# Bias and tap vectors loaded as rows and turned by TensorE, the last MLP tile column done half by half, and the diagonal matrices built later on VectorE, in a fused SSM-convolution and token-MLP kernel

## The chip, the cores and the metric

The kernel runs on one core of one Trainium2 chip (trn2). The metric is the device time of one execution in microseconds (us), lower is better. Before the change the median of three runs was 204.59 us (204.25 to 204.87). All results were correct against the reference. The profiled span is the time from the first to the last instruction; the device time is 1.9 us longer than the span (205.34 against 203.4 for the profile of before), so a microsecond of span is a microsecond of time.

## The reference, cut to what matters

```python
# S = 2048, D = 640, F = 1536, bf16
k_shift = sum over 4 taps of k_pad[:, t:t+S, :] * shift_k[:, 3-t]
kv      = k_shift * v
y       = causal convolution of kv with ssm_k over S (rfft, product, irfft) + kv * ssm_D
a       = q * y
h       = layernorm(x)             # x = q
b       = (gelu(h^T @ w1 + b1) @ w2 + b2)^T
g       = sigmoid((x * gate_w).sum(-1))
out     = g * a + (1 - g) * b
```

The small tensors of the change are `shift_k` (640 x 4 taps), `b1` (1536), `b2` (2048) and `gate_w` (640).

## The kernel before

The transforms are matrix products with a sine table `FTB`. TensorE first transposes `ssm_k` (`ident,ssm`), then transforms it (`wT,FTB`), makes the shifted `k` by products with diagonal matrices of the taps (`DG,KT`), transforms the products `k_shift * v` (`vkv,FTB` for the first half of the sequence, `kv,FTB` for the second), and does the MLP (`X,ring`, then `GT,W`) between and after these. ScalarE moves results out of PSUM. VectorE does layernorm, the products and the additions between transforms. GpSimd has two small operations for each group of four layernorm tiles. There are four PSUM slots.

No order is written down: operations are added to a list scheduler inside the program, with modelled durations, and it decides, once, when the program is built, in which order each engine gets its instructions. The chip runs the engines asynchronously in this fixed order. So a small edit (another assumed DMA rate) can move instructions on every engine.

The small loads, and the product that makes `DG`:

```python
for hk in range(2):
    ssm_load(hk)
small(gwb[:, :], dr(gate_w, 0, [[0, 128], [1, D]]), 128 * 1280, "QA")            # QA: ScalarE's DMA queue
small(shk[:, :, :], dr(A_shift_k, 0, [[4, 128], [512, ND], [1, 4]]), 5120, "QA", noncontig=True)
small(Drow[:, :], dr(A_ssm_D, 0, [[0, 1], [1, D]]), 1280, "QA")
for hk in range(4):
    x_load(hk)
ssm_load(2)
ssm_load(3)
small(b1t[:, :], dr(B_b1, 0, [[1, 128], [128, FT]]), 3072, "SP", noncontig=True, chain=True)
small(b2t[:, :].rearrange("p (a b) -> p a b", a=4), dr(B_b2, 0, [[4, 128], [512, 4], [1, 4]]), 4096, "SP", noncontig=True, chain=True)
# ... w1, k transposes ...
tt("DVE", DG[:, :, :, :].rearrange("p a b c -> p (a b) c"), V(ident, 0, [[0, 20], [1, 128]]), V(shk, 0, [[1, 20], [0, 128]]), ALU.mult, mode=1)
```

Layernorm for one group of four tiles (`STATS_ACT` groups, whose sums ScalarE makes, cut):

```python
def ln_tile(hk, p):
    t = 4 * hk + p
    xs = X[:, hk, p, :]
    # bn_stats twice, bn_aggr -> mv[:, t, :]            (DVE)
    stt("DVE", junk[1][:, :], xs, 1.0, gwb[:, :], ALU.mult, ALU.mult, acc=gpre[:, t:t + 1])   # the gate's sum

def ln_apply(hk):
    r = slice(4 * hk, 4 * hk + 4)
    ts("POOL", vtmp[:, r], mv[:, r, 1], 1e-5, None, ALU.add)
    tt("POOL", rstd[:, r], vtmp[:, r], V(cst, 1, [[0, 4]]), ALU.pow)
    for p in range(4):
        ts("DVE", X[:, hk, p, :], X[:, hk, p, :], mv[:, t, 0:1], rstd[:, t:t + 1], ALU.subtract, ALU.mult, mode=4, extra=0.17)

for h in range(2):
    # ... transposes and transforms of ssm half h ...
    for kt in range(2):
        for p in range(4):
            ln_tile(2 * h + kt, p)
        ln_apply(2 * h + kt)
    if h == 0:
        mixing(C[0], SS, 0, fine=True)       # additions between transforms, DVE
    else:
        mixing(C[1], C[0], 0)
```

The second MLP product, and the output of a pair of tiles:

```python
for p in range(4):
    vt = _VT("mlp")
    for a in range(3):
        items = []
        for ft in range(4 * a, 4 * a + 4):
            for ci in range(2):
                items.append((chk(ci), V(W2h, ft * 512 + p, [[4, 128]]), GT[:, ft, 320 * ci:320 * ci + 320], ft == 0, ft == FT - 1))
        mms(vt, items, prio=2 * 10 ** 6 + 4 * (4 * n_ + p) + a, name="m2")
    act(O1[:, hk, p, :].rearrange("p (a b) -> p a b", a=2), two, ACT.Identity, bias=c2[:, t:t + 1], scale=omg[:, t:t + 1], vt=vt, name="o1")
# ...
tt("DVE", ov, cg[:, :, :], ov, ALU.add)
dma(dr(out, (1024 * h + p) * D, [[4 * D, 128], [512 * D, 2], [1, D]]), ov, 256 * 1280, sem="out")
```

## Time and profile before

| | before (first profile) |
|---|---|
| time, median of 3 runs | 204.59 us |
| time of the profiled execution | 205.34 us |
| span of the profiled execution | 203.4 us |
| first matmul | 7.38 us |
| statistics begin on VectorE | 11.66 us |
| second-half kv transform begins on TensorE | 79.13 us |
| TensorE unbroken | 68.91 to 199.0 us |
| from TensorE's end to the span's end | 4.4 us |

From the page of the profile of before: busy time of the engines, the DMA rate in 40 equal slices (one is 5.1 us), and the chain that ended last.

```profile
PE 187.5 (92%) x1374; PEld 136.8 (67%) x1374; DVE 183.0 (90%) x202; ACT 103.2 (51%) x143; POOL 20.8 (10%) x25
...
GB/s 104 355 401 213 311 200 210 198 358 297 183 253 58 0 3 0 0 73 168 174 0 45 265 2 124 163 373 195 196 258 214 366 80 0 48 141 73 0 193 68
...
PE 86%; ACT 8%; DMA 3%; issue 0%; DVE 0%
```

TensorE (PE) and VectorE (DVE) are busy for almost the same time, 187.5 and 183.0 us. The chain says which of the two the end waited for: TensorE, for 86% of the span. VectorE appears in it only with the last addition (0.82 us), but with 183 us of work it cannot be far behind; the chain shows the last constraint and not the second to last. The fourth slice, 213 GB/s among slices of 355 and 401, is the time of the 2- and 8-byte elements of `b1` and `b2`.

The end of the chain of waits of before, in order of time (start, length, what):

```profile
65.97 1.28 ACT L651
...
67.27 0.79 ACT GT L651
...
68.17 0.60 ACT C_84 L651
...
68.91 130.09 PE pp L293 x960
...
199.02 0.89 ACT O_99 L651
...
199.93 0.82 DVE O_99 L613
```

TensorE's last stop before its long run ends at 68.91: it waits for a PSUM slot behind ScalarE's table load (1.28 us at 65.97) and what follows it. From there 960 recorded matmuls run without a gap, 130.09 / 960 = 0.1355 us each. Whatever comes after 68.91 on TensorE is full, so the end can only move if TensorE's last stop ends earlier, if fewer matmuls lie behind that stop, or if the tail (here ScalarE's eviction of 0.89, VectorE's addition of 0.82, and the output's transfer) gets shorter.

The timeline of before around the second-half kv transform (start, length, engine, line, operation, out<-in):

```profile
75.87 3.42 PE L293 MATMUL pp<-X,ring_80 128*128 128x320 bf16 x24
76.98 1.48 DVE L613 TENSOR_TENSOR kv_93<-ksh_95,v_92 128x2560 bf16<-128x2560 bf16 x1
...
79.13 1.11 PE L293 MATMUL pp<-kv_93,FTB 128*128 128x320 bf16 x7
```

VectorE's second kv product ends at 78.46, and TensorE reaches the transform that reads it at 79.13. So VectorE has a lead of 0.67 us here.

The timeline of before around the second layernorm group:

```profile
26.08 1.43 DVE L613 TENSOR_TENSOR SS<-C_82 128x2560 bf16<-128x2560 bf16 x1
...
26.25 1.35 POOL L623 TENSOR_SCALAR vtmp<-mv 128x4 f32<-128x4 f32 x1 [4.97 <-DVE mv L817]
27.69 1.04 POOL L613 TENSOR_TENSOR rstd<-vtmp,cst 128x4 f32<-128x4 f32 x1
...
28.77 1.51 DVE L624 TENSOR_SCALAR X<-X,mv,rstd 128x640 bf16<-128x640 bf16 x4 [1.25 <-POOL rstd L613]
```

The bracket is idle time ahead of an instruction and who ended it: VectorE waits 1.25 us for GpSimd's `rstd`.

### The profile page before, as it was taken

Reading aid. Unit: us, or ns where it says so; the run is one execution under the profiler, and the core shown is the slowest. Engines: PE = TensorE matmul, PEld = TensorE weight load, DVE = VectorE, ACT = ScalarE, POOL = GpSimd, SP = SyncE. Lnnn points to the kernel's source line nnn. Section 1 sums busy time; section 2 is a strip of 40 time slices with the busy share of each in tenths; the row PEclk is TensorE's granted clock in tenths of the full one; section 3 lists DMA queues with packets and bytes.
Section 4 is the critical chain, followed back from the end, with each engine's and each line's share of the span. In section 5 each row is a group of like instructions: output and inputs, shape, how many; then the busy total and the mean of one; then the engine's idle time right before and its main releaser. Section 6 shows DMA issues by size and latency. Waiting matters only on the chain.

```text
span 203.4 us, 3261 instructions
## 1 busy us (share of the span) xinstructions
PE 187.5 (92%) x1374; PEld 136.8 (67%) x1374; DVE 183.0 (90%) x202; ACT 103.2 (51%) x143; POOL 20.8 (10%) x25
## 2 busy tenths in 40 slices
PE   0479989999998999999999999999999999999991
PEld 0446556577654677777777777788888887777770
DVE  8799979998997999999999999999999992799651
ACT  4697988966378765883111211131322314643741
POOL 1002040402043500000000004004000000000000
PEclk9999999999999999999999999999999999999999
DMA  4998999999891000025501807995996920142051
GB/s 104 355 401 213 311 200 210 198 358 297 183 253 58 0 3 0 0 73 168 174 0 45 265 2 124 163 373 195 196 258 214 366 80 0 48 141 73 0 193 68
DMA packets 37904, 32.37 MB, mean 159 GB/s; under 512 B 18305, under 2 KB 35330, under 8 KB 37890
## 3 DMA queue, kind: packets, MB, share of 16 engines
q1 hardware_dynamic: 36000, 29.37, 49.4%
q0 software_dynamic: 1088, 2.62, 8.2%
q10 hardware_dynamic: 802, 0.17, 0.6%
q8 instruction: 11, 0.18, 0.3%
q14 instruction: 3, 0.02, 0.0%
HBM read 23.25 MB, written 2.62 MB: 127 GB/s over the span
## 4 chain that ended last, share of the span: by engine, by line
PE 86%; ACT 8%; DMA 3%; issue 0%; DVE 0%
PE pp L293 86%; DMA ssm<-in_A_ssm_k_dram 3%; ACT wT L651 3%; ACT C_84 L651 2%; ACT FTB L651 1%; ACT C_82 L651 1%; ACT L651 1%; ACT O_99 L651 0%; DVE O_99 L613 0%; ACT GT L651 0%; ACT gth L651 0%
## 5 line engine op out<-in xcount | busy, mean ns | idle before, releaser
L293 PE MATMUL pp<-X,ring_80 128*128 128x320 bf16 x256 | 36.9, 299 | 0.0
L293 PEld LDWEIGHTS pp<-X,ring_80 128*128 128x128 bf16 x256 | 25.0, 98 | 9.7
L651 ACT ACTIVATE O_99<-pp,c_66,omg 128x640 bf16<-128x640 f32 x16 | 14.2, 884 | 34.1 <-PE pp L293 34.1
L293 PE MATMUL pp<-GT,W_1_98 128*128 128x320 bf16 x192 | 27.2, 299 | 0.0
L293 PE MATMUL pp<-GT,W_0_97 128*128 128x320 bf16 x192 | 26.4, 299 | 0.0
L651 ACT ACTIVATE GT<-pp,b1f 128x640 bf16<-128x640 f32 x12 | 9.5, 794 | 30.6 <-PE pp L293 30.6
L293 PEld LDWEIGHTS pp<-GT,W_0_97 128*128 128x128 bf16 x192 | 21.8, 114 | 4.3
L293 PEld LDWEIGHTS pp<-GT,W_1_98 128*128 128x128 bf16 x192 | 21.7, 114 | 4.5
L293 PE MATMUL pp<-wT,FTB 128*128 128x320 bf16 x128 | 20.8, 321 | 0.1
L293 PE MATMUL pp<-X,ring_81 128*128 128x320 bf16 x128 | 17.6, 299 | 0.0
L293 PEld LDWEIGHTS pp<-wT,FTB 128*128 128x128 bf16 x128 | 11.9, 104 | 8.3 <-ACT C_83 L651 1.7
L293 PE MATMUL pp<-ident,ssm 128*128 128x128 bf16 x80 | 8.5, 266 | 8.5 <-DMA ssm<-in_A_ssm_k_dram 7.4
L293 PEld LDWEIGHTS pp<-X,ring_81 128*128 128x128 bf16 x128 | 12.5, 98 | 4.9
L815 DVE BATCH_NORM_STATS2 stats<-X 128x6 f32<-128x320 bf16 x32 | 13.7, 466 | 0.0
L293 PEld LDWEIGHTS pp<-ident,ssm 128*128 128x128 bf16 x80 | 6.6, 129 | 10.4 <-DMA ssm<-in_A_ssm_k_dram 8.0
L651 ACT ACTIVATE C_84<-pp 128x640 bf16<-128x640 f32 x16 | 10.5, 701 | 5.1 <-PE pp L293 5.1
L631 DVE SCALAR_TENSOR_TENSOR junk_75<-X,gwb 128x640 bf16<-128x640 bf16 x16 | 12.9, 808 | 0.0
L651 ACT ACTIVATE C_85<-pp 128x640 bf16<-128x640 f32 x16 | 10.1, 708 | 4.1 <-PE pp L293 4.1
L293 PE MATMUL pp<-vkv_91,FTB 128*128 128x320 bf16 x64 | 10.6, 301 | 1.1 <-ACT C_84 L651 1.1
L651 ACT ACTIVATE wT<-pp 128x640 bf16<-128x640 f32 x16 | 10.0, 730 | 2.2 <-PE pp L293 2.2
L651 ACT ACTIVATE C_82<-pp 128x640 bf16<-128x640 f32 x16 | 10.1, 735 | 1.9 <-PE pp L293 1.9
L651 ACT ACTIVATE C_83<-pp 128x640 bf16<-128x640 f32 x16 | 9.9, 774 | 0.6 <-PE pp L293 0.6
(103 smaller groups left out, 301.9 us busy)
## 6 DMA issues: line engine op xcount, KB each, us to landing
ring_80<-in_B_w_dram SPq DMA_DIRECT2D x8, 512.0 KB, 5.2
W_0_97<-in_B_w_dram SPq DMA_DIRECT2D x4, 768.0 KB, 9.5
W_1_98<-in_B_w_dram SPq DMA_DIRECT2D x4, 768.0 KB, 8.0
ssm<-in_A_ssm_k_dram SPq DMA_DIRECT2D x4, 640.0 KB, 10.5
X<-in_A_q_dram SPq DMA_DIRECT2D x4, 640.0 KB, 10.3
out_dram<-O_99 SPq DMA_DIRECT2D x8, 320.0 KB, 2.3
ring_81<-in_B_w_dram SPq DMA_DIRECT2D x4, 512.0 KB, 8.9
vkv_91<-in_A_v_dram SPq DMA_DIRECT2D x2, 640.0 KB, 5.7
```

Of the source, the lines that this page charges most:

```text
L293: ins = self.nc.tensor.matmul(ps_ap, lhsT=lhsT, rhs=rhs, start=start, stop=stop, skip_group_check=True)
L631: eng, lambda e: e.scalar_tensor_tensor(out=o, in0=a, scalar=sc, in1=b, op0=op0, op1=op1, accum_out=acc),
L651: return T.op("ACT", lambda e: e.activation(o, src, func, **kw), rr + [src], ww)
L815: SC.add("DVE", 0.46, (lambda o, i: lambda s: T.op("DVE", lambda e: e.bn_stats(o, i), [i], [o]))(o, i), [i], [o])
```

## The change

Its intent: the tiny-element loads of `b1`, `b2` and the taps become a few contiguous rows that TensorE transposes (nine small matmuls into one PSUM slot, one eviction to `cc`). `gwb` (160 KB) leaves the head of ScalarE's DMA queue and goes behind the first X block. `DG` is built from `cc`, no longer ahead of all statistics but behind those of the eighth tile, ahead of the first mixing. The assumed DMA rate of the scheduler goes from 280 to 320. The last MLP column is computed half by half, so that less is left to do after the last matmul. Cut to its core:

```diff
-        def dma(o, i, nbytes, stream="SP", prio=None, sem=None, rate=280.0, chain=False, **kw):
+        def dma(o, i, nbytes, stream="SP", prio=None, sem=None, rate=320.0, chain=False, **kw):
 ...
-        small(gwb[:, :], dr(gate_w, 0, [[0, 128], [1, D]]), 128 * 1280, "QA")
-        small(shk[:, :, :], dr(A_shift_k, 0, [[4, 128], [512, ND], [1, 4]]), 5120, "QA", noncontig=True)
         small(Drow[:, :], dr(A_ssm_D, 0, [[0, 1], [1, D]]), 1280, "QA")
-        for hk in range(4):
+        small(rows[0:5, 0, :], dr(A_shift_k, 0, [[512, 5], [1, 512]]), 5120, "QA")
+        small(rows[0:4, 1, :], dr(B_b2, 0, [[512, 4], [1, 512]]), 4096, "QA")
+        small(rows[0:12, 2, 0:128], dr(B_b1, 0, [[128, 12], [1, 128]]), 3072, "QA")
+        x_load(0)
+        dma(gwb[:, :], dr(gate_w, 0, [[0, 128], [1, D]]), 128 * 1280, chain=True)
+        for hk in range(1, 4):
             x_load(hk)
         ssm_load(2)
         ssm_load(3)
-        small(b1t[:, :], dr(B_b1, 0, [[1, 128], [128, FT]]), 3072, "SP", noncontig=True, chain=True)
-        small(b2t[:, :].rearrange("p (a b) -> p a b", a=4), dr(B_b2, 0, [[4, 128], [512, 4], [1, 4]]), 4096, "SP", noncontig=True, chain=True)
 ...
-        tt("DVE", DG[:, :, :, :].rearrange("p a b c -> p (a b) c"), V(ident, 0, [[0, 20], [1, 128]]), V(shk, 0, [[1, 20], [0, 128]]), ALU.mult, mode=1)
+        vt = _VT("cv")
+        items = []
+        for j in range(4):
+            items.append(((lambda s, j=j: s[:, 5 * j:5 * j + 5]), V(rows, j, [[4, 128]], pn=5), ident[0:5, 0:5], True, True))
+        for p in range(4):
+            items.append(((lambda s, p=p: s[:, 20 + 4 * p:24 + 4 * p]), V(rows, 512 + p, [[4, 128]], pn=4), ident[0:4, 0:4], True, True))
+        items.append(((lambda s: s[:, 36:48]), rows[0:12, 2, 0:128], ident[0:12, 0:12], True, True))
+        mms(vt, items, name="cst")
+        act(cc[:, :], lambda s: s[:, 0:48], ACT.Copy, vt=vt, name="cc")
 ...
             if h == 0:
+                tt("DVE", DG[:, :, :, :], V(ident, 0, [[0, 5], [0, 4], [1, 128]]), shkf, ALU.mult, mode=1)
                 mixing(C[0], SS, 0, fine=True)
 ...
+                last_ = n_ == 3 and p == 3
+                order = [(ft, ci) for ci in range(2) for ft in range(FT)] if last_ else [(ft, ci) for ft in range(FT) for ci in range(2)]
 ...
+                    if last_:
+                        act(O1[:, hk, p, 320 * a:320 * a + 320], chk(a), ACT.Identity, bias=c2[:, t:t + 1], scale=omg[:, t:t + 1], vt=vt, name="o1")
 ... (the last pair of output tiles: addition and output DMA in pieces)
```

What the diff does not show is what the scheduler makes of it. Comparing the instruction orders of the two kernels: on TensorE one 14-matmul piece of the second-half `DG,KT` products goes ahead of the first-half (`vkv`) transforms; these 64 matmuls, which had MLP matmuls between them, become one block; and 48 instead of 80 MLP matmuls lie ahead of the second-half kv transform.

More of the change, by code (lines that the diff above doesn't have):

```diff
@@ L555, in _build @@
         DG = alloc("DG", [128, ND, 4, 128], BF16)
-        shk = alloc("shk", [128, ND, 4], BF16)
+        cc = alloc("cc", [128, 48], F32)
         stats = alloc("stats", [128, 16, 12], F32)
@@ L566, in _build @@
         c2 = alloc("c2", [128, 16], F32)
-        b2t = alloc("b2t", [128, 16], BF16)
-        b1t = alloc("b1t", [128, FT], BF16)
-        b1f = alloc("b1f", [128, FT], F32)
         cst = alloc("cst", [128, 2], F32)
@@ L589, in _build @@
         ksh = [alloc(f"ksh{i}", [128, 4, D], BF16, at=base_of(GT) + 5120 * (1 + i)) for i in range(2)]
+        rows = alloc("rows", [12, 3, 512], BF16, at=base_of(GT))
         pint = alloc("pint", [128, 4, 2, 2, 256], I32, at=base_of(ring[1]))
@@ L759, in _build @@
                 scale=-(2.0 * math.pi / 4096.0) * (1.0 - 1e-6), name="sin")
-        tt("DVE", DG[:, :, :, :].rearrange("p a b c -> p (a b) c"), V(ident, 0, [[0, 20], [1, 128]]), V(shk, 0, [[1, 20], [0, 128]]), ALU.mult, mode=1)
+        vt = _VT("cv")
[7 more added lines that the diff above has]
+        act(cc[:, :], lambda s: s[:, 0:48], ACT.Copy, vt=vt, name="cc")
+        b1f = cc[:, 36:48]
+        b2f = V(cc, 20, [[1, 4], [4, 4]])
+        shkf = V(cc, 0, [[1, 5], [5, 4], [0, 128]])
         def transp(h, p, kt):
@@ L847, in _build @@
                 mixing(C[1], C[0], 0)
-        SC.add("POOL", 0.3, lambda s: T.op("POOL", lambda e: e.tensor_copy(b1f[:, :], b1t[:, :]), [b1t[:, :]], [b1f[:, :]]), [b1t[:, :]], [b1f[:, :]])
         gate_op = act(gth[:, :], gpre[:, :], ACT.Tanh, scale=0.5)
@@ L852, in _build @@
         ts("POOL", omg[:, :], gth[:, :], -0.5, 0.5, ALU.mult, ALU.add)
-        tt("POOL", c2[:, :], omg[:, :], b2t[:, :], ALU.mult)
+        tt("POOL", c2[:, :].rearrange("p (a b) -> p a b", a=4), omg[:, :].rearrange("p (a b) -> p a b", a=4), b2f, ALU.mult)
         memset("POOL", KT[0][:, :, 12:16], 0.0)
@@ L925, in _build @@
                 mms(vt, items, prio=10 ** 6 + 4 * ft + hk, name="m1")
-            g_ = act(GT[:, ft, :].rearrange("p (a b) -> p a b", a=2), two, ACT.Gelu_apprx_tanh, bias=b1f[:, ft:ft + 1], vt=vt, prio=0, name="gelu")
+            g_ = act(GT[:, ft, :].rearrange("p (a b) -> p a b", a=2), two, ACT.Gelu_apprx_tanh, bias=cc[:, 36 + ft:37 + ft], vt=vt, prio=0, name="gelu")
             if ft == 0:
@@ L945, in _build @@
                 t = 4 * hk + p
-                for a in range(3):
+                last_ = n_ == 3 and p == 3
+                order = [(ft, ci) for ci in range(2) for ft in range(FT)] if last_ else [(ft, ci) for ft in range(FT) for ci in range(2)]
+                na = 2 if last_ else 3
+                for a in range(na):
                     items = []
-                    for ft in range(4 * a, 4 * a + 4):
-                        for ci in range(2):
-                            items.append((chk(ci), V(W2h, ft * 512 + p, [[4, 128]]), GT[:, ft, 320 * ci:320 * ci + 320], ft == 0, ft == FT - 1))
+                    for ft, ci in order[a * (24 // na):(a + 1) * (24 // na)]:
+                        items.append((chk(ci), V(W2h, ft * 512 + p, [[4, 128]]), GT[:, ft, 320 * ci:320 * ci + 320], ft == 0, ft == FT - 1))
                     mms(vt, items, prio=2 * 10 ** 6 + 4 * (4 * n_ + p) + a, name="m2")
-                act(O1[:, hk, p, :].rearrange("p (a b) -> p a b", a=2), two, ACT.Identity, bias=c2[:, t:t + 1], scale=omg[:, t:t + 1], vt=vt, name="o1")
+                    if last_:
+                        act(O1[:, hk, p, 320 * a:320 * a + 320], chk(a), ACT.Identity, bias=c2[:, t:t + 1], scale=omg[:, t:t + 1], vt=vt, name="o1")
+                if not last_:
+                    act(O1[:, hk, p, :].rearrange("p (a b) -> p a b", a=2), two, ACT.Identity, bias=c2[:, t:t + 1], scale=omg[:, t:t + 1], vt=vt, name="o1")
         A0 = {0: (C[2], 2), 1: (C[1], 0)}
@@ L1027, in inverse @@
                 tt("DVE", cg[:, :, :], cg[:, :, :], (q_lo if h == 0 else q_hi)[:, :, p, :], ALU.mult)
-                tt("DVE", ov, cg[:, :, :], ov, ALU.add)
-                dma(dr(out, (1024 * h + p) * D, [[4 * D, 128], [512 * D, 2], [1, D]]), ov, 256 * 1280, sem="out")
+                if h == 0 and p == 3:
+                    tt("DVE", O1[:, 0, p, :], cg[:, 0, :], O1[:, 0, p, :], ALU.add)
+                    dma(dr(out, p * D, [[4 * D, 128], [1, D]]), O1[:, 0, p, :], 128 * 1280, sem="out")
+                    for ci in range(2):
+                        ov = O1[:, 1, p, 320 * ci:320 * ci + 320]
+                        tt("DVE", ov, cg[:, 1, 320 * ci:320 * ci + 320], ov, ALU.add)
+                    ov = O1[:, 1, p, :]
+                    dma(dr(out, (512 + p) * D, [[4 * D, 128], [1, D]]), ov, 128 * 1280, sem="out")
+                else:
+                    tt("DVE", ov, cg[:, :, :], ov, ALU.add)
+                    dma(dr(out, (1024 * h + p) * D, [[4 * D, 128], [512 * D, 2], [1, D]]), ov, 256 * 1280, sem="out")
         ncg = [0]
```

## The prediction

> **What bounds it now.** The chain of waits puts 86% of the 203.4 us span on TensorE. Five places lie outside its steady work: (1) nothing runs until ssm block 0 lands (first matmul 7.38 us); (2) to 14.4 us it waits on ScalarE; (3) 52.5 to 69 us is uneven: PE and ScalarE alternate on vkv transforms, and the table load (1.28) with what follows holds PE until 68.91; (4) from 68.91 it never stops: 130.1 us for 960 recorded matmuls, 0.1355 each; (5) tail: PE ends at 199.0, then 0.88 eviction, 0.82 add, about 2.65 output DMA. VectorE is a near co-bottleneck: from 11.66 to 169 us it idles under 5 us in all (timeline), and its second kv product (76.98 to 78.46) barely precedes the kv transform (79.13).
>
> **The change, costed.**
> - b1, b2 and taps arrive as rows instead of 2- and 8-byte elements. In the DMA records these elements drop the traffic from about 0.4 MB/us to 0.58 MB in 17.3 to 20.7 us: about 2.5 us lost. That moves w1, the k transposes and v about 3 us earlier. The Trainium skill, "DMA: Bandwidth & Descriptors", Specifications, wants at least 512 B for line rate; this trace agrees. PE does not wait for w1 now, so almost none of that is direct gain.
> - gwb (160 KB, landed 5.16) and the taps (640 packets, landed 8.90) no longer compete with ssm blocks 0 and 1 (7.34, 9.44). Estimate: these land 0.6 to 1 us earlier, X block 0 (11.03) likewise.
> - Added: nine tiny matmuls and a 128x48 eviction, about 0.3 us on the path. Net for the front: 0.3 to 0.8 us.
> - The DG product stays at about 2.8 us (2.83 before). It moves from before the statistics (VectorE 8.92 to 11.66) behind the eighth tile's statistics. Statistics start about 1.5 us earlier, DG costs 2.8 later but fills the 1.25 us wait for rstd: VectorE is about even by 41 us.
> - The order on PE changes (scheduler): one 14-matmul kv chunk of the second half goes ahead of the vkv transforms; these then run as one block with three slots; the table load falls behind the last kv eviction. That removes the stalls of (3). In exchange only 48, not 80, MLP matmuls lie ahead of the kv transform. PE would reach it about 73.3 us; VectorE's second kv product (two operations earlier in its order, and earlier by the front's gain) ends about 73.7. From there 912 matmuls x 0.1355 = 123.6, so PE ends near 197.3 instead of 199.0.
> - Risk: that early chunk needs the second half's k transposes (landed from 52.7; expected about 49.5 to 50.5), about when PE gets there.
> - Tail: only half a tile is left after the last matmul: eviction 0.88 to about 0.61, add 0.82 to about 0.3, half the output. About 1.0 us saved.
>
> **Sum.** 1.7 + 1.0 = 2.7 us: 204.59 to about 201.9 us, 1.3% faster. Range 200.0 to 203.6. Faster by over 2%: 0.17; within 2%: 0.80; slower: 0.03.
>
> **What would show it.** First matmul about 6.7; statistics begin near 10; no low-traffic stretch at 17 to 21; no PE wait on the table load; kv transform starting 73 to 75, waiting for VectorE's kv product; PE unbroken after it to about 197; last matmul to end about 3.4 instead of 4.4.
>
> **What would make it wrong.** Better: X and v landing earlier still, so VectorE runs ahead and the kv transform starts at 72. Worse: PE stalls over 2 us on the early k-transpose chunk, VectorE loses more than it gains by the moved DG, or an inverse transform reaches PE before VectorE's result (margins by my count 2 to 5 us).

## The result, and the profile after

| | before | after |
|---|---|---|
| time, median of 6 runs | 204.57 us (204.13 to 204.87) | 203.05 us (202.93 to 203.36) |
| ratio after / before | | 0.993, 95% interval 0.9916 to 0.9945 |
| span of the profiled execution | 203.4 us | 201.0 us |
| first matmul | 7.38 | 5.59 |
| statistics begin on VectorE | 11.66 | 8.97 |
| kv transform goes on without a break | 79.13 | 73.91 |
| TensorE ends | 199.0 | 197.9 |
| from there to the span's end | 4.4 | 3.1 |

The change gained 1.5 us: inside 2%, inside the predicted range, and a little over half of the 2.7 us predicted.

From the page of the profile of after, the same lines:

```profile
PE 187.1 (93%) x1383; PEld 136.2 (68%) x1383; DVE 183.4 (91%) x204; ACT 102.9 (51%) x145; POOL 24.8 (12%) x24
...
GB/s 158 344 406 348 284 160 201 305 344 231 221 176 0 0 3 0 0 3 234 183 0 34 273 10 103 160 360 218 166 273 341 359 14 0 130 68 65 0 138 126
...
PE 62%; DVE 25%; POOL 5%; DMA 4%; issue 2%; SPq 1%; ACT 0%
```

The busy times are as before. The fourth slice of the DMA rate has risen from 213 to 348: the tiny elements are gone. And the chain has turned over: from 86% TensorE to 62%, with 25% VectorE and 5% GpSimd. POOL's busy time rose by 4 us with one instruction less: a copy into `KT` took 5.02 us instead of 2.47, and the `vtmp` of the second layernorm group 2.69 instead of 1.35. The second of these is explained below.

The chain of waits of after, its last pieces (start, length, what):

```profile
58.51 2.70 POOL vtmp L621
...
61.28 1.05 POOL rstd L611
...
62.35 1.51 DVE X L622 x4
...
68.04 1.48 DVE kv L611
...
72.37 1.50 DVE kv L611
...
73.91 124.00 PE pp L293 x910
...
197.93 0.63 ACT O L649
...
198.58 0.33 DVE O L611
```

Followed back, this chain runs through VectorE's statistics to the landing of `gwb` at 9.99 us. So between 10 and 74 us it is VectorE, with GpSimd's two operations in it, that decides; TensorE takes over at 73.91 with 910 recorded matmuls left (0.1363 us each) and never stops again.

The timeline of after around the second-half kv transform:

```profile
68.86 3.42 PE L293 MATMUL pp<-X,ring 128*128 128x320 bf16 x24
...
72.12 0.43 PE L293 MATMUL pp<-kv,FTB 128*128 128x320 bf16 x2
72.37 1.48 DVE L611 TENSOR_TENSOR kv<-ksh,v 128x2560 bf16<-128x2560 bf16 x1
...
73.91 2.08 PE L293 MATMUL pp<-kv,FTB 128*128 128x320 bf16 x14 [1.36 <-DVE kv L611]
```

TensorE arrives at 72.12, does the two matmuls that need only the first kv product, and stands for 1.36 us until VectorE's second product is done at 73.85. In before VectorE had 0.67 us to spare at the same place.

The timeline of after around the second layernorm group:

```profile
23.65 2.77 DVE L611 TENSOR_TENSOR DG<-ident,cc 128x2560 bf16<-128x2560 bf16 x1
23.82 2.69 POOL L621 TENSOR_SCALAR vtmp<-mv 128x4 f32<-128x4 f32 x1 [6.57 <-DVE mv L827]
26.59 1.04 POOL L611 TENSOR_TENSOR rstd<-vtmp,cst 128x4 f32<-128x4 f32 x1
27.66 1.15 DVE L622 TENSOR_SCALAR X<-X,mv,rstd 128x640 bf16<-128x640 bf16 x3 [1.25 <-POOL rstd L611]
```

`vtmp` now lasts 2.69 us and ends 0.09 us after the `DG` product. The same operation took 0.24 us at 15.88 us of this execution, when no such VectorE operation ran beside it. So the `DG` product did not fill VectorE's wait for `rstd`: it held up the very operation that the wait is for, and the wait behind it is 1.25 us as before. The Trainium skill, "SBUF — State Buffer", section "SBUF: two separate sides", describes this: VectorE with two inputs in SBUF and a GpSimd operation that reads SBUF share one pair of ports, whoever starts first has it for the whole instruction, and the other "fully blocks". This trace agrees, here and at 58.51 (2.69 us beside a VectorE operation of 2.77).

### The profile page after: what moved, and what is told of

Same layout as the page of the kernel before. It is cut to its first block, busy times and chain, and to the rows that moved or that the text cites. A ratio compares the mean times of both kernels' runs of the same rounds, so it can differ in the third digit from the quotient of the medians.

```text
span 201.0 us, 3282 instructions
## 1 busy us (share of the span) xinstructions
PE 187.1 (93%) x1383; PEld 136.2 (68%) x1383; DVE 183.4 (91%) x204; ACT 102.9 (51%) x145; POOL 24.8 (12%) x24
## 4 chain that ended last, share of the span: by engine, by line
PE 62%; DVE 25%; POOL 5%; DMA 4%; issue 2%; SPq 1%; ACT 0%
PE pp L293 62%; DVE stats L825 5%; DVE junk L629 5%; DVE C L611 5%; DMA gwb<-in_gate_w_dram 4%; POOL vtmp L621 3%; DVE X L622 3%; DVE SS L611 3%; POOL rstd L611 2%; DVE kv L611 1%; DVE vkv L611 1%; DVE mv L827 1%; SPq L267 1%; ACT O L649 0%; DVE O L611 0%
## 5 line engine op out<-in xcount | busy, mean ns | idle before, releaser
L293 PE MATMUL pp<-X,ring 128*128 128x320 bf16 x384 | 53.6, 299 | 0.0
L293 PE MATMUL pp<-GT,W 128*128 128x320 bf16 x384 | 52.8, 299 | 0.0
L293 PEld LDWEIGHTS pp<-GT,W 128*128 128x128 bf16 x384 | 43.4, 113 | 8.9 <-issue 0.2
L611 DVE TENSOR_TENSOR C<-C 128x2560 bf16<-128x2560 bf16 (+1 forms) x28 | 49.0, 1769 | 0.3
L293 PEld LDWEIGHTS pp<-X,ring 128*128 128x128 bf16 x384 | 37.5, 98 | 14.5
L649 ACT ACTIVATE C<-pp 128x640 bf16<-128x640 f32 x64 | 39.3, 752 | 7.1 <-PE pp L293 7.0
L649 ACT ACTIVATE O<-pp,c,omg 128x640 bf16<-128x640 f32 (+1 forms) x17 | 14.5, 853 | 36.7 <-PE pp L293 36.7
L611 DVE TENSOR_TENSOR tm<-C,C 128x5120 bf16<-128x5120 bf16 x8 | 22.2, 2817 | 0.0
L293 PE MATMUL pp<-wT,FTB 128*128 128x320 bf16 x128 | 19.8, 314 | 0.0
L293 PE MATMUL pp<-DG,KT 128*128 128x256 bf16 (+3 forms) x140 | 18.1, 288 | 0.6 <-DMA KT<-in_A_k_dram 0.6
L611 DVE TENSOR_TENSOR C<-tm 128x2560 bf16<-128x2560 bf16 x12 | 17.4, 1484 | 0.1
```

The lines of the kernel that those rows point to most:

```text
L293: ins = self.nc.tensor.matmul(ps_ap, lhsT=lhsT, rhs=rhs, start=start, stop=stop, skip_group_check=True)
L611: return SC.add(eng, d, lambda s: T.op(eng, lambda e: e.tensor_tensor(o, a, b, op), [a, b], [o]), [a, b], [o], prio=prio, name="tt")
L649: return T.op("ACT", lambda e: e.activation(o, src, func, **kw), rr + [src], ww)
```

## The experiments

Two theories stood against each other. **T1**: in the changed kernel VectorE's chain, from the landing of X and `gwb` to the second kv product, decides when TensorE can go on for good; after that every matmul counts. Then faster TensorE work in front gains nothing, and more TensorE work ahead of the wait, or a shorter VectorE chain, gains at once. **T2**, the rival: TensorE's own front (cold clock, first data, its stalls) and the DMA traffic still set the time, and the wait of 1.36 us is only incidental. Each edit below is against the kernel after unless it says otherwise. Times are medians; "before" is the kernel before in the same rounds (medians 204.69, 204.54 and 204.51 in the three batches). First batch: e_before to e_rate. Second: e_lnord to e_lnord_fill8. Third: the last four. The kernel after was not run again in these batches, so a difference against its 203.05 us is one between batches. Taken from the ratios instead of the medians, such differences come out up to 0.3 us apart (e_fill8 1.3 us instead of 1.0, e_actq 1.1 instead of 1.25, e_taps 0.0 instead of 0.2), so a difference of a few tenths should not be relied on.

### e_before: the kernel before, again

No edit. It measures the noise, and gives a second profile of before.

> The kernel before, unchanged, once more. In the changed kernel time less span is 1.95 us in every run; in the profiled execution of before it is also 1.94 (205.34 less 203.4), but that execution was 0.77 us above the median of before. Theory (the profile that I predicted from was a long execution): time again 204.6, ratio 1.000 +-0.002, new profiled span 202.4 to 202.9, kv transform about 78.3 instead of 79.13. Rival (span and time are not tied together, the profile was typical): new profiled span again 203.2 to 203.6.

Measured: 204.72 us, ratio 1.0003 (0.998 to 1.0026). The profiled execution took 204.79 us with a span of 202.9; TensorE ended at 198.45, and the kv transform began at 78.59 (79.13 in the first profile). So the first profile was of an unusually long execution, and "199.0" was not before's typical end. The two also differ in how long TensorE's 320-column matmuls took 471 ns rather than 299: until 18.45 us in the first profile, 16.88 in this one. This goes together with the longer execution; I have not shown that it is the whole of it.

### e_tailonly: the kernel before with the tail's part alone

```diff
 against the kernel before
+                last_ = n_ == 3 and p == 3
+                order = [(ft, ci) for ci in range(2) for ft in range(FT)] if last_ else [...]
 ... (all of the change's edits of the last column and the last output pair, and no others)
```

> The kernel before with only the tail of the change (last MLP tile half by half, output of that pair in two transfers); TensorE's order stays the same. Theory: the tail is critical from end to end, so its whole saving arrives: 1.2 us faster (time 203.3 to 203.5), last matmul to end of span about 3.1 instead of 4.4. Rival (the tail gives less since the last transfer's fixed time dominates): 0.5 us or less.

Measured: 203.67 us, ratio 0.9949 (0.9931 to 0.9968), 1.02 us less than before. The tail in its timeline:

```profile
198.52 0.62 ACT L651 ACTIVATE O<-pp,c,omg 128x320 bf16<-128x320 f32 x1 [1.01 <-PE pp L293]
199.17 0.32 DVE L613 TENSOR_TENSOR O<-cgb,O 128x320 bf16<-128x320 bf16 x1 [1.31 <-ACT O L651]
```

The eviction fell from 0.88 to 0.62 us and the addition from 0.82 to 0.32, and the span ends 3.1 us after TensorE instead of 4.4. This part of the change is worth 1.0 of the 1.5 us. All the rest of the change together is worth 0.5.

### e_fill8: eight more MLP matmuls ahead of the kv transform

```diff
+                    if first_a is not None and name == "A" and h == 1:
+                        first_a.append(fo)                # matmul groups of the second-half kv transform
 ...
+                if (ft, hk) == (1, 2):
+                    for fo in first_a:
+                        fo.after.add(mo)                  # none of them ahead of this MLP group
```

> The changed kernel with eight MLP matmuls (1.08 us) moved ahead of the second half's kv transform, where TensorE waits 1.36 us for VectorE's kv product (73.91); nothing else moves. Theory T1 (VectorE's chain sets the moment at which TensorE goes on, and TensorE never stops after it): wait shrinks to about 0.3 us, PE ends 1.0 to 1.1 us earlier, time about 202.0, ratio to before 0.987 to 0.989. Rival T2 (the end is set later on, by VectorE's products before the inverse transforms or by the output): time stays 203.0.

Measured: 202.07 us, ratio 0.9866 (0.9845 to 0.9886), 1.0 us less than after. The timeline:

```profile
72.67 1.48 DVE L611 TENSOR_TENSOR kv<-ksh,v 128x2560 bf16<-128x2560 bf16 x1
73.64 2.65 PE L293 MATMUL pp<-kv,FTB 128*128 128x320 bf16 x16
```

TensorE arrives at 73.64 instead of 72.12 and the wait has shrunk to 0.14 us (VectorE ends at 74.15, and the first two matmuls do not need it). In this profile TensorE ended at 197.11, 0.8 us earlier than in that of after. Nothing was taken away from any engine; eight matmuls, 1.08 us of TensorE's work at 0.1355 each, were put where TensorE stood idle. That is T1's prediction, in size too (202.07 us measured, about 202.0 expected).

### e_rate: the kernel after with the scheduler's old DMA rate

```diff
-        def dma(o, i, nbytes, stream="SP", prio=None, sem=None, rate=320.0, chain=False, **kw):
+        def dma(o, i, nbytes, stream="SP", prio=None, sem=None, rate=280.0, chain=False, **kw):
```

> The changed kernel with the scheduler's assumed transfer rate put back from 320 to 280: same instructions and transfers, but TensorE gets the order of before (80 instead of 48 MLP matmuls ahead of the kv transform, kv chunk not ahead of the vkv transforms). T1: VectorE delivers the kv product at about 77.5 to 78.2 in its old order, TensorE arrives at about 77.7, then 880 matmuls x 0.1355: end within 0.5 us of the changed kernel (202.6 to 203.5). Rival T3 (the new order on TensorE is where the gain before the tail comes from): 0.8 us or more slower than the changed kernel, that is 203.8 or more; opposite rival (the new order costs): 202.3 or less.

Measured: 202.95 us, ratio 0.9914 (0.9897 to 0.9931). The intervals of this ratio and that of after (0.993) overlap. TensorE has before's order again: vkv transforms broken up, 80 MLP matmuls ahead of the kv transform. The chain of waits:

```profile
64.69 1.28 ACT L649
...
73.06 124.64 PE pp L293 x917
```

and the timeline of the same kernel:

```profile
75.71 1.48 DVE L611 TENSOR_TENSOR kv<-ksh,v 128x2560 bf16<-128x2560 bf16 x1
77.85 2.34 PE L293 MATMUL pp<-kv,FTB 128*128 128x320 bf16 x16
```

VectorE's product is done at 77.19 and TensorE comes at 77.85, so here VectorE is not the limit; I had expected it to be. TensorE itself is, through its alternation with ScalarE and ScalarE's table load at 64.69. The time is the same as after's within the intervals, by another limit. The edit puts back VectorE's old order with TensorE's (three more additions stand ahead of its second kv product, as in before), so it does not separate the two. Together the new orders, which my prediction credited with the larger part of the gain, gained nothing in this kernel: TensorE's stalls went, and a wait for VectorE came in their place.

### e_lnord: gate products behind the group's statistics

```diff
-            stt("DVE", junk[1][:, :], xs, 1.0, gwb[:, :], ALU.mult, ALU.mult, acc=gpre[:, t:t + 1])
+        def gate_tile(hk, p):
+            t = 4 * hk + p
+            stt("DVE", junk[1][:, :], X[:, hk, p, :], 1.0, gwb[:, :], ALU.mult, ALU.mult, acc=gpre[:, t:t + 1])
 ...
                 for p in range(4):
                     ln_tile(2 * h + kt, p)
+                for p in range(4):
+                    gate_tile(2 * h + kt, p)
                 ln_apply(2 * h + kt)
```

Now the group's statistics are complete four gate products earlier, and VectorE has useful work while GpSimd makes `rstd`.

> The changed kernel with the gate's products (two-input VectorE operations) of each group of four tiles moved behind the group's statistics, so that other VectorE work stands between the last aggregate and the normalisation while GpSimd computes rstd; TensorE's order unchanged. In the changed kernel VectorE waits 1.25, 0.83 and 1.24 us for rstd ahead of the kv product. T1 (VectorE's chain sets the kv transform's start): second kv product ends near 71.0 to 72.5 instead of 73.85, TensorE goes on at about 72.2, time 201.4 to 201.9. Rival 1 (the end is not set by this chain): 203.0. Rival 2 (GpSimd is held off by whatever two-input operation VectorE runs, so the waits just move): waits for rstd still above 2 us in all, time 202.5 to 203.1.

Measured: 201.5 us (201.09 to 202.84), ratio 0.9855 (0.9826 to 0.9884), 1.5 us less than after. VectorE's waits for `rstd` fell from 3.3 us to 0.4. The timeline shows how, although GpSimd is held as before:

```profile
21.97 2.82 DVE L611 TENSOR_TENSOR DG<-ident,cc 128x2560 bf16<-128x2560 bf16 x1
22.21 3.48 POOL L611 TENSOR_TENSOR rstd<-vtmp,cst 128x4 f32<-128x4 f32 x1
24.71 0.82 DVE L629 SCALAR_TENSOR_TENSOR junk<-X,gwb 128x640 bf16<-128x640 bf16 x1
...
25.73 0.45 DVE L622 TENSOR_SCALAR X<-X,mv,rstd 128x640 bf16<-128x640 bf16 x1 [0.19 <-POOL rstd L611]
```

`rstd` takes 3.48 us instead of 1.04, beside the `DG` product (to 24.79) and the gate product after it (to 25.53), and costs VectorE 0.19 us, because that gate product was left to do meanwhile. The second kv product then ends at 72.6, TensorE does not wait for it, and the kv transform begins at 73.52. The profiled execution was the slowest of the six, and in it the next limit shows: TensorE waits 2.5 us for the second half's k transposes. In the five others (spans 199.2 to 200.1) the waits are not known.

### e_strided: the strided bias loads added back, unused

```diff
+        small(b1t[:, :], dr(B_b1, 0, [[1, 128], [128, FT]]), 0, "SP", noncontig=True, chain=True)
+        small(b2t[:, :].rearrange("p (a b) -> p a b", a=4), dr(B_b2, 0, [[4, 128], [512, 4], [1, 4]]), 0, "SP", noncontig=True, chain=True)
```

> The changed kernel, which also loads b1 and b2 in the old way, 2 and 8 bytes at a time, at the old place of the queue, into tiles that nobody reads; order of all engines unchanged. It costs the queue about 2.5 us, so the second half's k transposes land at about 50.8 to 51.7 instead of 48.3 to 49.2. T1 (off the path but for little, VectorE's chain has 1.4 us to give): TensorE's wait before the early kv chunk grows from 1.2 to about 3.5 us, kv transform starts at 74.0 to 74.7 instead of 73.9, time 203.1 to 203.9. Rival (these loads were a direct cost): 2 us or more slower, 205 or more.

Measured: 203.43 us, ratio 0.9952 (0.9917 to 0.9988), 0.4 us more than after, which is within the noise. The low-traffic stretch is back in its DMA rate, at 17.4 to 19.8 us (down to 17 GB/s in one slice of 0.6 us). TensorE waited 1.18 us for the first block of `w1` at 21.34, where it did not wait in after. The second half's k transposes landed only 1.0 to 1.1 us later than in after; I had expected 2.5. The kv transform went on at 73.90, after TensorE had waited 0.36 us instead of 1.36 for VectorE. So TensorE's lead shrank by the delay, and the time hardly changed: as T1 has it, most of what the rows save lay in front of a wait.

### e_warm: 30 matmuls at the start, to warm TensorE's clock

```diff
+        wvt = _VT("cv")
+        mms(wvt, [((lambda s: s[:, 0:128]), ident[:, :], ident[:, :], True, True)] * 30, name="warm")
```

> The changed kernel with 30 matmuls of ident by ident on TensorE ahead of everything (their result is never read), while it waits for the first ssm block. In the profiles TensorE's matmuls take 471 ns instead of 299 until 16.3 us (changed) or 16.9 to 18.5 us (before). Expected: matmuls at 299 ns from the first transforms at about 14 us on, first transforms 0.8 to 1.0 us ahead. T1 (VectorE sets the moment): that lead is lost at the kv transform, time 202.8 to 203.1. Rival (TensorE's front counts in full): 202.0 to 202.3.

Measured: 203.18 us, ratio 0.9935 (0.9907 to 0.9963), the same as after. TensorE did get ahead: its forward transforms began at 12.42 instead of 13.90. But this was not what I had expected: ten of the 320-column matmuls still lasted more than 320 ns (most of them 471, to 15.17), as many as in after, and the granted clock reads 0.50 from 11.6 to 14.8. What got faster were the transposes of `ssm_k` well ahead of them (219 ns each for the first ones instead of 311). The timeline where TensorE first needs `w1` (`ring`), and at the kv transform:

```profile
21.17 1.26 PE L293 MATMUL pp<-X,ring 128*128 128x320 bf16 x8 [1.83 <-DMA ring<-in_B_w_dram]
...
72.31 1.48 DVE L611 TENSOR_TENSOR kv<-ksh,v 128x2560 bf16<-128x2560 bf16 x1
...
73.85 2.08 PE L293 MATMUL pp<-kv,FTB 128*128 128x320 bf16 x14 [1.37 <-DVE kv L611]
```

The last line is after's line (73.91, wait 1.36). But VectorE is not what took the lead of 1.5 us: TensorE lost it at 21.17 to a wait of 1.83 us for `w1`, which landed at 21.12 (20.04 in after), and came to the kv transform at 72.05, as in after (72.12). So this run does not decide between T1 and T2 as it was meant to. It shows only that VectorE's second product ended at 73.79 (73.85 in after) with TensorE's faster start, so that a lead that had lasted would have ended in the same wait. T1 rests on e_fill8 and e_lnord.

### e_lnord_fill8: both mends

The edits of e_lnord and e_fill8 together.

> Both mends together: gate products behind the statistics and eight MLP matmuls ahead of the kv transform. T1: the kv transform is then TensorE's own: no wait for VectorE there, kv transform starts at about 73.3 with 1.08 us of MLP already done, time 201.4 to 201.9, no better than either mend alone by more than 0.5 us. Rival (savings add up): 200.7 or less.

Measured: 201.88 us, ratio 0.9861 (0.9839 to 0.9884), no better than either alone (0.9855, 0.9866). In its profile TensorE has no wait for VectorE, and the k transposes hold it for 0.5 and 0.34 us. The two mends treat the same wait; once it is gone, the second does nothing.

### e_actq: `gwb` and the 8-byte taps back at the head of ScalarE's DMA queue

```diff
-        dma(gwb[:, :], dr(gate_w, 0, [[0, 128], [1, D]]), 128 * 1280, chain=True)
 ... (its place in the schedule is kept, so that the order on the engines stays)
+        T.dma("ACT", gwb[:, :], dr(gate_w, 0, [[0, 128], [1, D]]), "gwq")
+        T.dma("ACT", shk[:, :, :], dr(A_shift_k, 0, [[4, 128], [512, ND], [1, 4]]), "shkq", noncontig=True)
         SC.emit()
+        T.op("POOL", lambda e: e.tensor_copy(shk2[:, :, :], shk[:, :, :]), [shk[:, :, :]], [shk2[:, :, :]])
```

The taps loaded so are not used (the rows' taps still are); a copy at the very end reads them.

> The changed kernel with the two transfers of before at the head of ScalarE's queue again: gwb (instead of behind X block 0) and the taps 8 bytes at a time (into a tile that only a copy at the very end reads); the order of all computing instructions unchanged. X block 0 should land at 10.5 to 11.1 us instead of 8.95, so the statistics start 1.5 to 2.1 us later. T1 (VectorE's chain from the first X block to the kv product has no slack): second kv product and kv transform later by the same amount (75.4 to 76.0), time 204.5 to 205.1, no better than before. Rival (the start is absorbed later on): 203.0 to 203.5.

Measured: 204.3 us, ratio 0.9983 (0.9964 to 1.0003), 1.25 us more than after. X block 0 landed at 10.76 instead of 8.95, the statistics began at 10.78, the second kv product ended at 75.42 instead of 73.85, and:

```profile
75.48 2.08 PE L293 MATMUL pp<-kv,FTB 128*128 128x320 bf16 x14 [1.37 <-DVE kv L613]
```

The delay of 1.8 us at the first X block arrives as 1.57 us at the kv transform, and TensorE's wait is the same 1.37: TensorE is late by as much as VectorE, and 0.99 us of that was a wait for VectorE's second vkv product at 54.37. The time moved by 1.25. So with the changed kernel's order on the engines, the place of two loads in a queue is worth 1.25 us.

### e_taps: the 8-byte taps alone

The same edit without `gwb`.

> The same with only the taps' 640 packets of 8 bytes put back at the head of ScalarE's queue, gwb stays behind X block 0. T1: X block 0 lands 0.4 to 1.2 us later than in the changed kernel and the kv transform follows by the same amount, time 203.5 to 204.2. Rival (the small packets cost nothing): 203.0.

Measured: 203.28 us, ratio 0.9932 (0.9913 to 0.9951), 0.23 us more than after by the medians and none by the ratio. X block 0 landed at 9.42 (0.47 later) and the kv transform went on at 74.17 (0.26 later). So of the 1.25 us the taps make 0.2 at most, and the 160 KB of `gwb` ahead of X the rest, unless the two together cost more than each alone; `gwb` alone was not run.

### e_lnord_rate: e_lnord with the old DMA rate

The edits of e_lnord and e_rate together.

> Gate products behind the statistics, and the scheduler's rate at 280, which puts more MLP matmuls ahead of the kv transform and takes the early kv chunk (and with it the wait for the k transposes, 1 to 2.5 us in the other profiles) back. T1: neither VectorE nor the transposes hold TensorE; what is left is the alternation with ScalarE in the vkv transforms. Time 200.8 to 201.6. Rival (that alternation and the table load cost as much as the wait for the transposes): 201.6 to 202.6.

Measured: 202.67 us, ratio 0.9895 (0.987 to 0.9919). TensorE's order is again like before's, with the vkv transforms broken up, but now 88 MLP matmuls lie ahead of the kv transform, not 80. The transform begins at 78.82, with VectorE's second product done at 76.83, two microseconds before. With VectorE mended and TensorE in this order, TensorE is the limit. Against e_lnord (201.5), which has the new orders, this is 1.2 us slower; the intervals of the two ratios just overlap. So the new orders, worth nothing in the kernel after, seem to be worth about 1 us once VectorE's wait is gone.

### e_lnord_rate_warm: the same with the 30 matmuls at the start

The edits of e_lnord, e_rate and e_warm together.

> The same with the 30 idle matmuls at the start, which gave nothing in the changed kernel (203.18 against 203.05) although its first transforms began 1.5 us earlier. T1: now TensorE is not held by VectorE, so a lead at the start can arrive: 0.4 to 1.0 us faster than without them. Rival (the lead is lost in any case, to ScalarE): same within 0.3 us.

Measured: 201.25 us (201.06 to 202.06, 5 runs), ratio 0.9839 (0.9815 to 0.9862), span 199.1. The same edit gained nothing in e_warm and 1.4 us here (202.67 to 201.25), where TensorE is the limit; I had expected 0.4 to 1.0. The two are not a clean pair: here TensorE first needed `w1` at 21.25, when it had just landed (21.20), and did not wait, while in e_warm it came earlier and lost its lead there. Here TensorE's transforms began at 12.64 instead of 13.88, with 5 slow matmuls instead of 9. Its timeline:

```profile
73.70 1.48 DVE L611 TENSOR_TENSOR kv<-ksh,v 128x2560 bf16<-128x2560 bf16 x1
77.16 2.34 PE L293 MATMUL pp<-kv,FTB 128*128 128x320 bf16 x16
```

The kv transform begins 1.66 us earlier than in e_lnord_rate. This is the fastest median and beats both kernels; against e_lnord (201.5) the difference is within noise.

## Why the prediction was right or wrong

The time (203.05) lies in the range, and "within 2%" was right. The gain (1.5 us) was overestimated by 1.2. Point by point:

- **The baseline, the largest error.** "PE ends near 197.3 instead of 199.0" and "204.59 to about 201.9 us" mix two executions. 199.0 belongs to the profiled execution, which took 205.34 us; the 2.7 us were subtracted from the median, 204.59. Subtracted from the time of the execution they were read from, they give 205.34 - 2.7 = 202.64 us, and 203.05 was measured. So 0.75 of the 1.15 us by which the predicted time was too low is this one step, and 0.4 is all the rest. e_before confirms it: its TensorE ended at 198.45. With a typical span of before (204.57 - 1.94 = 202.6) and its tail of 4.4, TensorE's typical end is 198.2, and the gain ahead of the tail was 198.2 - 197.9 = 0.3 us in place of 1.7. Counted by times it is 0.5 (1.52 in all, less the 1.02 of e_tailonly); the two counts agree within the intervals.
- **The kv transform.** "VectorE's second kv product ... ends about 73.7" was right, but partly by luck (see below): it ended at 73.85, and the transform went on at 73.91. "PE would reach it about 73.3 us" was wrong: TensorE came at 72.12 and stood for 1.36 us. The predicted wait for VectorE was there, three times as long as the 0.4 us that my two numbers implied. From there the prediction had 912 matmuls in 123.6 us; the trace has 910 in 124.0, which puts TensorE's end at 197.9.
- **Why the order on TensorE gained nothing.** The prediction saw that the stalls of 52 to 69 us would go, and they did: the vkv transforms ran from 52.53 to 61.9 without a stop. But the time of e_rate, which has the old orders, equals after's, so the new orders together are worth nothing here. The removal of the stalls was turned into the wait of 1.36 us, at a place where 32 fewer MLP matmuls (32 x 0.1355 = 4.3 us) lay ahead of the transform. The transform went on 4.7 us earlier than in e_before (78.59 to 73.91), but 4.3 us of that is work pushed behind it.
- **`DG` and the `rstd` wait.** "DG costs 2.8 later but fills the 1.25 us wait for rstd" was half wrong. Its length was right (2.77). But GpSimd's `vtmp` was held for as long (2.69), and the wait of 1.25 us came after it all the same. The trace of before had shown this already: there `vtmp` took 1.35 us beside an addition of 1.43, and the wait behind it was the same 1.25. "VectorE is about even by 41 us" was right in its sum: the second vkv product began at 51.27 in after, and at 51.31 and 50.77 in the two profiles of before, although the statistics had begun 2.7 and 3.1 us earlier. The front's gain on VectorE went into `DG` in its new place and into waits for `rstd` (3.3 us in all, 2.5 in before).
- **How the second kv product still comes 4 us earlier** (72.37; 76.98 and 76.44 in the profiles of before): three of the additions that stood ahead of it now stand behind it (about 4.2 us). This is order, not less work. The prediction had two operations and the front's gain. Two are 2.8 us, so about 2 us of its step from 78.46 to 73.7 had to come from the front; of that only 0.4 us arrived at the fourth layernorm group (62.73 to 62.35, and nothing against e_before's 62.19). One operation too few and a gain that did not come cancelled each other.
- **The front** was underestimated. The prediction had the first matmul at about 6.7 and the statistics near 10; they came at 5.59 and 8.97. e_actq shows what the larger part of it, the queue's head, is worth in the changed kernel: 1.25 us, by way of VectorE. Put together with e_tailonly: e_actq, which has the tail's 1.0 us and everything else but this, is only 0.2 us faster than before (204.3 against 204.51). So the tail gave 1.0, the queue's head 1.25, and the remaining parts together (`DG`'s new place, the new orders, the rows of the biases) cost about 0.8 (an estimate, good to some 0.3 us). This sum takes the parts as additive, which e_lnord_fill8 shows they need not be.
- **The rows for `b1` and `b2`**: "almost none of that is direct gain" held (0.4 us, within noise, e_strided). The Trainium skill's figure in "DMA: Bandwidth & Descriptors", section "Specifications" (at least 512 B for line rate) agrees with the trace in kind. The predicted "about 3 us earlier" for what follows was too much as an effect of the biases: put back in e_strided they delayed the second half's k transposes by 1.0 to 1.1 us. (The prediction's "0.58 MB in 17.3 to 20.7 us" is too high: the records of that profile add up to 0.41 MB.) "PE stalls over 2 us on the early k-transpose chunk" did not happen: it waited 0.28 us twice.
- **The tail**: "About 1.0 us saved" is what e_tailonly measured (1.02). The stretch from "last matmul to end", predicted at "about 3.4", was 3.1.

What stays open: whether the longer stretch of 471 ns matmuls is all that made the first profile of before long; what TensorE's and VectorE's new orders do separately; what `gwb` alone and `DG`'s new place alone cost; and what the k transposes do in the faster executions of e_lnord.

## What to carry to other kernels

When two engines are busy for nearly the same time, removing stalls on the one that the chain names can merely move the wait to the other, as it did here; look up how much lead the second engine has at each place where they meet (0.67 us here), and do not book more than that. Fill a wait that remains with work that is due later anyway (eight matmuls moved: 1.0 us), or shorten what is waited for (1.5 us); here doing both bought nothing more. And read the baseline's times and its profile from the same execution, or correct by the difference, before you subtract microseconds from a median.

## What the Trainium skill lacked or had wrong

- "TensorE: Matmul & The Clock Gate", section "Single matmul latency": for 320 columns its warm formula, (398 + N) / 2.4, gives 299 ns, and the trace shows 299. The cold one, (219 + N) / 1.2, gives 449 ns; the traces show 471 (before) and 474 (after).
- The same page, section "What's actually happening", says that the number of cold matmuls varies from run to run. The two profiles of before agree: 16 and 9 matmuls of over 320 ns.
- "ScalarE: Activation LUTs", section "What ACT_TABLE_LOAD costs", gives 1.283 us for the load and 1.38 for a drain with it. The load took 1.28 us here; the drain does not show: in before ScalarE's work ahead of the load ended at 65.95, the load began at 65.97, and the next activation began at 67.27.
- "DMA: Bandwidth & Descriptors" gives the minimum size for line rate, and not what a load of tiny elements does to the transfers beside it. Here 2,048 elements of 2 and 8 bytes in one queue took the rate of the whole core from about 350 down to 5 GB/s, and below 70 for 1.8 us, in before; yet the same loads added to after delayed later k transposes by only 1.0 to 1.1 us.
- "SBUF — State Buffer", section "Who interferes with whom", has the rule that mattered most. No page gives a duration for the small case that it decides: a GpSimd operation of 128 x 4 elements, 0.24 us by itself, takes 2.69 us beside a VectorE product of 2,560 columns.
